# A leaky rectifier in place of a scaled copy in the decoding of float64 weights, and one VectorE instruction less

## The chip, the cores and the metric

The kernel runs on one core of one Trainium2 chip. The metric is the device time of one execution in microseconds (us), as the median of several runs. The engines are named as in the profile: PE is TensorE (PEld its weight loads), DVE is VectorE, ACT is ScalarE, POOL is GpSimd, SP is SyncE, which only issues transfers here.

## The reference

A windowed attention with a linear bias per head is followed by a feed-forward network with an approximate GELU. The weights of the network are float64; everything else is float32.

```python
# q, k, v: (8 batches, 8 heads, 576 positions, 64), float32
scores = scale * np.matmul(q, k.transpose(0, 1, 3, 2))
mask = (rel >= 0) & (rel < 128)              # rel = row - column
scores = np.where(mask, scores + bias[None], -1000000000.0)
attn = softmax(scores)                       # written out in the reference
out = np.matmul(attn, v)
x = out.transpose(0, 2, 1, 3).reshape(4608, 512)
h = x @ w_in                                 # (512, 2048), float64
g = h * (1.0 / (1.0 + np.exp(-1.702 * h)))
return g @ w_out                             # (2048, 512), float64
```

## The kernel before

**Feed-forward.** The 4608 rows of x are cut into 18 chunks of 256. The hidden width of 2048 is cut into 16 groups of 128. One step of a `Job` works on one chunk and one group: `up` multiplies x by a group of w_in into `h_ps` (line 553), ScalarE takes the tanh (line 558), VectorE makes g (line 559), ScalarE and GpSimd split g into a high and a low part, `gh` and `gl` (lines 562 and 563), and `down` multiplies these by a group of w_out into two accumulators `acc` (line 572). Each operand is held as a high part and the rest, so there are three products for one: 12 matmuls in `up`, 6 in `down`.

**Attention.** It runs as a pipeline of units; `tick` starts the next stage of several units. In the first two batches a unit is whole (`WholeUnit`): scores into `s_ps` and `sb_ps` (line 325), bias and row minimum on VectorE (line 352), exponentials on ScalarE (line 375), the sums' reciprocal `rec` on VectorE (lines 393 and 394), scaling of the probabilities `pb` by it on GpSimd and ScalarE (lines 403 and 400), transposes into `t_ps` (line 420), copies to `pw` (line 428), and the product with v into `x_ps` (line 477). `s_ps` has one buffer, so the next unit's scores wait until line 352 has read the last ones.

**Decoding.** The weights come in as float64, 32 tiles of 128x512 values: one of w_in and one of w_out for each of the 16 groups, in the order in which the groups are needed. `fetch` loads a tile through SP's queue (line 155). `decode` turns it into a float32 in `wc` and splits that into a high and a low part. A float64 is seen as two 32-bit words. The upper word, read as a float32, has the sign, the upper 8 bits of the 11-bit exponent, and then the other 3 bits of it and 20 of the fraction. ScalarE scales it by 2^-112 (line 211), which lowers the exponent field by 112; VectorE shifts the lower word right by 29 bits (line 212), shifts the scaled word left by 3 and joins the two (line 213): the exponent field then has the wanted value and the fraction 23 bits, but the sign has been shifted out. Line 214 takes the sign from the upper word and joins it. ScalarE rounds to the high part (line 217) and GpSimd subtracts for the low part (line 218). `wc` has three buffers, which it shares with another small tile.

**Order.** The program writes 24 steps in which the 32 tiles are decoded, at a pace that follows from when each group is needed, and mixes in the ticks of the attention. The order on each engine is then set by a scheduler that models each instruction's time. What is pinned keeps its written order: SP's loads, TensorE's idle matmuls at the start, and the first 8 decoded tiles. Each engine works through its queue in order, so an instruction that waits holds up all that stands behind it.

Of the kernel before, what the change touches and what calls it, by code (L numbers as in the profile page):

```python
# [8 lines left out]
F32 = mybir.dt.float32  # L9
# [4 lines left out]
AF = mybir.ActivationFunctionType  # L14
ALU = mybir.AluOpType
# [127 lines left out]
def tile_kernel(ctx: ExitStack, tc: tile.TileContext, q0, k0, v0, qT, kT, v, w_in, w_out, out):  # L143
    nc = tc.nc
# [58 lines left out]
    def decode(st, name, pin=lambda ins: ins):  # L203

        words = st.bitcast(I32).rearrange("p (m two) -> p m two", two=2)
        top, low = words[..., 1], words[..., 0]
        c = ffn.tile([P, 512], I32, name="wc", tag="o", bufs=3)

        pin(nc.scalar.activation(c.bitcast(F32), top.bitcast(F32), AF.Copy, scale=2.0 ** -112))
        pin(nc.vector.tensor_scalar(low, low, 29, None, ALU.logical_shift_right))  # L212
        pin(nc.vector.scalar_tensor_tensor(c, c, 3, low, ALU.logical_shift_left, ALU.bitwise_or))  # L213
        pin(nc.vector.scalar_tensor_tensor(c, top, -0x80000000, c, ALU.bitwise_and, ALU.bitwise_or))  # L214
        w = c.bitcast(F32)
        res = const.tile([P, 2, 512], F32R, name=name, tag=name)
        pin(nc.scalar.copy(res[:, 0], w))
        pin(nc.gpsimd.tensor_tensor(res[:, 1], w, res[:, 0].bitcast(F32), ALU.subtract))
        return res
# [425 lines left out]
    def decode_next():  # L645
        nonlocal halves
        g, ws = halves // 2, (w1, w2)[halves % 2]

        pin = [tc.keep_in_program_order] if halves < PINNED else []
        ws[g] = decode(ws[g], f"w{1 + halves % 2}_{g}", *pin)  # L650
        halves += 1
# [123 lines left out]
```

## Time and profile before

| | |
|---|---|
| time, median of 3 runs | 1074.23 us (1074.23 to 1074.42) |
| span of the profiled execution | 1072.5 us; the rest of its time, start and end outside the span, is not shown apart |
| mean granted clock of TensorE | 0.991 |
| PE busy | 1053.5 us, 98% of the span |
| DVE, ACT, POOL busy | 687.3, 595.2 and 610.8 us |
| line 214 | 32 instructions, 673 to 2394 ns, median 694, from 21.9 to 142 us |
| all of `decode` | 32 tiles, from 17.5 to 147 us |

Rows of busy time in a stretch read: start and end in us, length, then for each engine its busy time in us with the number of instructions, then the granted clock (1.00 is full speed), the share of the transfer engines that is busy, and GB/s. Rows in order of time read: start, length, engine, line, operation, output and inputs, and in brackets how long the engine was idle before it and what ended that. Rows by line give the shortest, median and longest duration in ns, and the first and the last start. Buffer numbers are left out of names there, so `rw` is any tile of raw weights.

### The profile page before, as it was taken

The page shows a single profiled execution, that of the slowest core. Times are in us where ns is not written, and L with a number is a line of the kernel's source. Part 1 is how long each engine was busy: PE and PEld are TensorE (multiplying, and loading weights), DVE is VectorE, ACT ScalarE, POOL GpSimd, SP SyncE. Part 2 cuts the span into 40 slices and gives each one's busy share as a digit, 9 for nine tenths or more (in the row PEclk, how much of TensorE's full clock was granted, in tenths as well). Part 3 has the DMA queues.
Part 4 walks back from the last instruction along what each step waited for, and adds up shares of the span by engine and source line. Part 5 has one row for each costly group of instructions (what it writes and reads, how often), then busy time and mean ns, then how long its engine had stood idle before and what let it go on. Part 6 is the DMA issues. An engine that isn't in the chain of part 4 may idle for free.

```text
span 1072.5 us, 21419 instructions
## 1 busy us (share of the span) xinstructions
PE 1053.5 (98%) x7041; PEld 931.5 (87%) x7041; DVE 687.3 (64%) x2149; ACT 595.2 (56%) x1811; POOL 610.8 (57%) x863
## 2 busy tenths in 40 slices
PE   9888999999999999999999999999999999999998
PEld 5656777899999999999999999999999999999987
DVE  6899843647896777654667668767877687413121
ACT  6869954546665565444555555655665556322222
POOL 3669954556675666554656557656666565323222
PEclk9889999999999999999999999999999999999999
DMA  8861112312223132202222213222222221000000
GB/s 309 305 231 54 44 30 75 83 38 77 75 80 85 51 86 75 62 16 67 58 76 54 70 53 90 75 60 71 82 65 85 57 77 28 20 2 20 1 21 20
DMA packets 88110, 78.45 MB, mean 73 GB/s; under 512 B 36800, under 2 KB 79296, under 8 KB 88000
## 3 DMA queue, kind: packets, MB, share of 16 engines
q1 hardware_dynamic: 82240, 67.14, 21.7%
q10 hardware_dynamic: 5760, 9.96, 2.5%
q8 instruction: 55, 0.90, 0.4%
q14 instruction: 55, 0.45, 0.1%
HBM read 67.63 MB, written 9.44 MB: 72 GB/s over the span
## 4 chain that ended last, share of the span: by engine, by line
PE 92%; DVE 4%; ACT 1%; DMA 1%; issue 0%; POOL 0%; SPq 0%; DVEq 0%; POOLq 0%; ACTq 0%
PE acc L572 37%; PE h_ps L553 37%; PE s_ps L335 5%; PE x_ps L500 5%; PE t_ps L443 4%; PE x_ps L477 1%; DVE wc L214 1%; DVE wc L213 1%; PE t_ps L420 1%; PE sb_ps L325 1%; DVE rw L212 1%; ACT pb L375 1%; PE s_ps L325 1%; DMA rw<-w_out 1%; DVE pb L352 0%; PE acc L189 0%
## 5 line engine op out<-in xcount | busy, mean ns | idle before, releaser
L563 POOL TENSOR_TENSOR gl<-g,gh 128x256 fp32r<-128x256 f32 x288 | 219.7, 763 | 284.1 <-ACT gh L562 220.0
L553 PE MATMUL h_ps<-xh,w 128*128 128x256 f32 x2304 | 370.2, 284 | 1.5 <-DVE g L559 1.0
L553 PEld LDWEIGHTS h_ps<-xh,w 128*128 128x128 f32 x2304 | 329.2, 189 | 33.2 <-DVE g L559 2.0
L572 PE MATMUL acc<-w,gh 128*128 128x512 f32 x1152 | 326.7, 401 | 0.5 <-ACT gh L562 0.5
L558 ACT ACTIVATE g<-h_ps 128x256 f32<-128x256 f32 x288 | 110.0, 382 | 237.5 <-PE h_ps L553 213.3
L559 DVE SCALAR_TENSOR_TENSOR g<-g,h_ps 128x256 f32<-128x256 f32 x288 | 119.4, 415 | 190.6 <-ACT g L558 189.3
L572 PEld LDWEIGHTS acc<-w,gh 128*128 128x128 f32 x1152 | 196.9, 189 | 28.2 <-ACT gh L562 1.1
L553 PE MATMUL h_ps<-xl,w 128*128 128x256 f32 x1152 | 196.1, 281 | 0.0
L562 ACT CAST gh<-g 128x256 fp32r<-128x256 f32 x288 | 116.5, 405 | 137.7 <-DVE g L559 127.0
L572 PE MATMUL acc<-w,gl 128*128 128x512 f32 x576 | 187.6, 401 | 0.1
L553 PEld LDWEIGHTS h_ps<-xl,w 128*128 128x128 f32 x1152 | 165.2, 189 | 6.7 <-issue 0.3
L313 POOL TENSOR_TENSOR K<-rk,K 128x384 fp32r<-128x384 f32 (+1 forms) x120 | 109.1, 909 | 75.0 <-ACT Q L293 14.3
L382 ACT ACTIVATE pb<-pb,mins 128x256 f32<-128x256 f32 (+2 forms) x216 | 105.0, 487 | 40.7 <-DVE mins L363 39.6
L572 PEld LDWEIGHTS acc<-w,gl 128*128 128x128 f32 x576 | 92.6, 189 | 10.5 <-issue 2.2
L407 DVE TENSOR_SCALAR pb<-pb,rec 128x256 f32<-128x256 f32 (+2 forms) x216 | 94.5, 473 | 3.3
L312 POOL TENSOR_TENSOR Q<-rq,Q 64x256 fp32r<-64x256 f32 (+1 forms) x120 | 82.8, 690 | 22.3 <-DVE g L559 3.3
L363 DVE CUSTOM_DVE_ANT_0 pb<-s_ps,bias 128x256 f32<-128x256 f32 (+3 forms) x240 | 85.7, 377 | 11.1 <-PE s_ps L335 9.8
L393 DVE TENSOR_SCALAR rec<-sums 128x2 f32<-128x2 f32 (+3 forms) x144 | 47.7, 331 | 57.6 <-ACT pb L382 52.9
L335 PE MATMUL s_ps<-K,Q 128*128 128x256 f32 (+1 forms) x432 | 80.2, 289 | 0.0
L311 DVE CAST K<-rk 128x384 fp32r<-128x384 f32 (+1 forms) x120 | 51.4, 428 | 44.6 <-PE s_ps L335 39.4
L462 DVE TENSOR_TENSOR pl<-t_ps,ph 128x512 fp32r<-128x512 f32 (+2 forms) x120 | 72.2, 604 | 8.3 <-ACT ph L456 4.5
L443 PE MATMUL t_ps<-ident,pb 128*128 128x128 f32 x408 | 73.9, 272 | 0.0
(69 smaller groups left out, 1354.9 us busy)
## 6 DMA issues: line engine op xcount, KB each, us to landing
rk<-kT SPq DMA_DIRECT2D x72, 192.0 KB, 2.5
rq<-qT SPq DMA_DIRECT2D x96, 128.0 KB, 2.4
out<-o ACTq DMA_DIRECT2D x36, 256.0 KB, 2.1
rw<-w_in SPq DMA_DIRECT2D x16, 512.0 KB, 6.2
rw<-w_out SPq DMA_DIRECT2D x16, 512.0 KB, 7.0
rk<-kT SPq DMA_DIRECT2D x48, 128.0 KB, 2.3
rv<-v SPq DMA_DIRECT2D x96, 64.0 KB, 2.0
rq<-q SPq DMA_DIRECT2D x16, 128.0 KB, 2.2
```

The costliest lines, as they stand in the source:

```text
L313: nc.gpsimd.tensor_tensor(K2, rk, K1.bitcast(F32), ALU.subtract)
L335: nc.tensor.matmul(u.s[:b.rows, e, b.first:b.end], u.Q[:, b.q0 - u.q0:b.q0 - u.q0 + b.rows], k[:, ko:ko + b.end - b.first], start=(z == 0) ...
L363: nc.vector.tensor_tensor_reduce(b.p[ra:rb, cs:b.end], u.s[ra:rb, e, cs:b.end], bias[head][ra:rb, cs:b.end], -SCALE, BIG, ALU.add, ALU.min ...
L382: nc.scalar.activation(live, live, AF.Exp, bias=u.mins[:b.rows, e:e + 1], scale=-1.0, accum_out=u.sums[:b.rows, e:e + 1],)
L407: nc.vector.tensor_scalar(live, live, u.rec[:rows, e:e + 1], None, ALU.mult)
L443: nc.tensor.transpose(u.t[:c.n, w:w + b.rows], b.p[:b.rows, col:col + c.n], ident[:b.rows, :b.rows])
L553: nc.tensor.matmul(h, w1[f][:, z, k * P:(k + 1) * P], x[:, k], start=(n == 0), stop=(n == len(ops) - 1))
L558: nc.scalar.activation(g, h, AF.Tanh, scale=0.851)
L559: nc.vector.scalar_tensor_tensor(g, g, 1.0, h, ALU.add, ALU.mult)
L562: nc.scalar.copy(gh, g)
L563: nc.gpsimd.tensor_tensor(gl, g, gh.bitcast(F32), ALU.subtract)
L572: nc.tensor.matmul(acc, g[:, t * P:(t + 1) * P], w2[f][:, z], start=(f == self.f0 and n == 0), stop=(f == self.f1 - 1 and n == 2))
```

## The change

ScalarE's first step uses a leaky rectifier instead of a copy: a positive word is scaled by 2^-112 as before, a negative one by 2^-112 times 2^32, so its exponent field is 32 higher. Shifted left by 3, this bit lands in the place of the sign. So the sign comes through the shift, and VectorE's third instruction is dropped.

```diff
-        pin(nc.scalar.activation(c.bitcast(F32), top.bitcast(F32), AF.Copy, scale=2.0 ** -112))
+        pin(nc.scalar.activation(c.bitcast(F32), top.bitcast(F32), AF.Prelu, scale=2.0 ** -112, alpha=2.0 ** 32))
         pin(nc.vector.tensor_scalar(low, low, 29, None, ALU.logical_shift_right))
         pin(nc.vector.scalar_tensor_tensor(c, c, 3, low, ALU.logical_shift_left, ALU.bitwise_or))
-        pin(nc.vector.scalar_tensor_tensor(c, top, -0x80000000, c, ALU.bitwise_and, ALU.bitwise_or))
         w = c.bitcast(F32)
```

Since the scheduler sets the order, other instructions move too. In the rows below an instruction is named by its line, operation, output and inputs; `rw_7_519` is a raw tile of group 7, and the last number only tells buffers apart (a group's tile of w_in has the lower one). After the change all lines behind 213 have a number lower by one: 352 is 351, 325 is 324, 553 is 552. A row of line 352 with the output `mins` alone reads out the row minimum.

VectorE before, around the wait for the weights of group 7 (43.5 us in the trace of before):

```order
L352 ISA pb,mins<-s_ps,bias_74 64x192
L352 ISA mins 64x1
L212 TENSOR_SCALAR rw_7_519<-rw_7_519 128x512
L213 SCALAR_TENSOR_TENSOR wc<-wc,rw_2_205 128x512
L393 TENSOR_SCALAR rec<-sums 128x4
L214 SCALAR_TENSOR_TENSOR wc<-rw_2_205,wc 128x512
L212 TENSOR_SCALAR rw_2_207<-rw_2_207 128x512
L394 RECIPROCAL rec<-rec 128x4
L212 TENSOR_SCALAR rw_7_521<-rw_7_521 128x512
L352 ISA pb,mins<-s_ps,bias_76 64x192
```

The same place after the change:

```order
L351 ISA pb,mins<-s_ps,bias_74 64x192
L351 ISA mins 64x1
L213 SCALAR_TENSOR_TENSOR wc<-wc,rw_2_205 128x512
L212 TENSOR_SCALAR rw_2_207<-rw_2_207 128x512
L212 TENSOR_SCALAR rw_7_517<-rw_7_517 128x512
L392 TENSOR_SCALAR rec<-sums 128x4
L393 RECIPROCAL rec<-rec 128x4
L212 TENSOR_SCALAR rw_7_519<-rw_7_519 128x512
L351 ISA pb,mins<-s_ps,bias_76 64x192
```

The steps on group 2 (line 213, and line 212 on its second tile) now stand ahead of line 212 on group 7, and line 214 is gone; behind that wait only the reciprocal and the second tile of group 7 are left ahead of the next reading of `s_ps`.

TensorE before, at the same time (from 43.2 us in the trace of before; `w_2_578` is the decoded first tile of group 2):

```order
L325 MATMUL s_ps<-rk,rq 64x192
L325 MATMUL sb_ps<-rk,rq 64x192
L477 MATMUL x_ps<-pw,VV 64x128 x2
L477 MATMUL x_ps<-pw,VV 64x256 x2
L477 MATMUL x_ps<-pw,VV 64x128 x2
L325 MATMUL s_ps<-rk,rq 64x192
L553 MATMUL h_ps<-xh,w_2_578 128x256 x4
L420 MATMUL t_ps<-ident,pb 128x128 x8
```

And after the change:

```order
L324 MATMUL s_ps<-rk,rq 64x192
L324 MATMUL sb_ps<-rk,rq 64x192
L476 MATMUL x_ps<-pw,VV 64x128
L324 MATMUL s_ps<-rk,rq 64x192
L552 MATMUL h_ps<-xh,w_2_573 128x256 x4
L419 MATMUL t_ps<-ident,pb 128x128 x2
L476 MATMUL x_ps<-pw,VV 64x128
L476 MATMUL x_ps<-pw,VV 64x256 x2
L476 MATMUL x_ps<-pw,VV 64x128 x2
L419 MATMUL t_ps<-ident,pb 128x128 x6
```

The third score product of this place has moved ahead of nearly all of the `x_ps` products, and the first products with the weights of group 2 with it.

VectorE before, from 59.3 us in the trace of before, behind a reciprocal that GpSimd waits for:

```order
L394 RECIPROCAL rec<-rec 64x2
L213 SCALAR_TENSOR_TENSOR wc<-wc,rw_3_260 128x512
L213 SCALAR_TENSOR_TENSOR wc<-wc,rw_4_318 128x512
L214 SCALAR_TENSOR_TENSOR wc<-rw_3_260,wc 128x512
L393 TENSOR_SCALAR rec<-sums 64x2
L212 TENSOR_SCALAR rw_11_739<-rw_11_739 128x512
L214 SCALAR_TENSOR_TENSOR wc<-rw_4_318,wc 128x512
L394 RECIPROCAL rec<-rec 64x2
L213 SCALAR_TENSOR_TENSOR wc<-wc,rw_4_320 128x512
L352 ISA pb,mins<-s_ps,bias_80 64x192
L352 ISA mins 64x1
L212 TENSOR_SCALAR rw_11_741<-rw_11_741 128x512
```

After the change, from the reciprocal of the same unit:

```order
L393 RECIPROCAL rec<-rec 64x2
L213 SCALAR_TENSOR_TENSOR wc<-wc,rw_4_320 128x512
L212 TENSOR_SCALAR rw_11_729<-rw_11_729 128x512
L351 ISA pb,mins<-s_ps,bias_80 64x192
L351 ISA mins 64x1
L392 TENSOR_SCALAR rec<-sums 64x2
L558 SCALAR_TENSOR_TENSOR g<-g,h_ps 128x256
L393 RECIPROCAL rec<-rec 64x2
L212 TENSOR_SCALAR rw_11_731<-rw_11_731 128x512
L213 SCALAR_TENSOR_TENSOR wc<-wc,rw_5_379 128x512
```

The two tiles of group 4 and the second of group 3 were decoded behind this reciprocal; now only one of line 213 and one of line 212 stand between it and the next unit's reading of `s_ps`.

## The prediction

> **What bounds the kernel now.** I read the busy shares first, then busy time by stretch, then the waits of TensorE, and last the instructions in order of time where it waits. All times are of one profiled execution with a span of 1072.5 us; the runs' median is 1074.23, so 1.7 us lie around the span and I take them as unchanged. The first fence is the page's first part, the second busy time in three stretches (start and end, length, then the busy time of each engine, the clock and the DMA share).
>
> ```profile
> PE 1053.5 (98%) x7041; PEld 931.5 (87%) x7041; DVE 687.3 (64%) x2149; ACT 595.2 (56%) x1811; POOL 610.8 (57%) x863
> ```
> ```profile
> 0.00:43.50 43.50, 39.17 (x261) 25.54 (x261) 32.37 (x123) 33.60 (x105) 20.54 (x30) 1.00 0.84 285
> 43.50:106.00 62.50, 53.71 (x310) 38.01 (x306) 57.68 (x130) 48.04 (x147) 49.80 (x37) 0.86 0.54 186
> 106.00:1072.50 966.50, 960.60 (x6474) 867.93 (x6474) 597.28 (x1898) 513.61 (x1561) 540.47 (x796) 1.00 0.20 56
> ```
> Over the span TensorE is the bound, but not in the middle row: there it stands idle for 62.50 - 53.71 = 8.8 us, while VectorE is busy for 57.68 of 62.50, and the clock is 0.86. That is where the weights are decoded beside the first attention and feed-forward steps. After 106 us TensorE is busy for 960.60 of 966.50, so what is won before 106 stays won. The same stretch cut into thirds, and below it the busy time of line 214's instructions alone (second number, with their count):
>
> ```profile
> 43.50:55.00 11.50, 8.99 (x47) 6.69 (x43) 7.68 (x24) 6.95 (x19) 8.94 (x6) 0.70 1.01 390
> 55.00:75.00 20.00, 16.21 (x88) 11.21 (x88) 19.87 (x36) 13.02 (x42) 14.40 (x10) 0.74 0.74 254
> 75.00:106.00 31.00, 28.51 (x178) 20.11 (x178) 30.13 (x72) 28.06 (x87) 26.46 (x21) 1.00 0.23 67
> ```
> ```profile
> 43.50:55.00 11.50, 1.37 (x2) 0.70 1.01 390
> 55.00:75.00 20.00, 7.29 (x6) 0.74 0.74 254
> 75.00:106.00 31.00, 9.07 (x9) 1.00 0.23 67
> ```
> The instruction that goes holds VectorE for 1.37 + 7.29 + 9.07 = 17.73 us there, in 17 of its 32 executions. In the last two thirds VectorE is never free (19.87 of 20, 30.13 of 31); in the first it is free for a third, and the DMA share of 1.01 says that weights are still arriving.
>
> The clock falls in whole blocks. Cut at 3.41 us, the rows are (TensorE's busy time is the second number, the clock the third from the right):
>
> ```profile
> 43.84:47.25 3.41, 1.84 (x17) 1.18 (x16) 3.41 (x14) 1.89 (x5) 1.35 (x2) 1.00 1.02 407
> 47.25:50.66 3.41, 2.46 (x12) 2.06 (x11) 3.26 (x10) 2.50 (x11) 3.41 (x2) 0.50 1.02 414
> 50.66:54.07 3.41, 3.41 (x13) 2.98 (x13) 0.70 (x1) 2.03 (x5) 3.41 (x4) 0.50 1.06 379
> ...
> 60.89:64.30 3.41, 1.53 (x17) 1.17 (x17) 3.41 (x9) 1.90 (x7) 3.41 (x2) 1.00 1.03 378
> 64.30:67.71 3.41, 3.40 (x14) 2.06 (x14) 3.41 (x3) 2.01 (x8) 3.36 (x4) 0.50 0.13 37
> 67.71:71.12 3.41, 2.16 (x6) 1.73 (x7) 3.41 (x7) 2.06 (x8) 1.62 (x1) 0.50 0.73 203
> 71.12:74.53 3.41, 3.41 (x21) 2.70 (x19) 3.34 (x5) 2.02 (x5) 2.37 (x2) 0.50 1.03 377
> ```
> Twice a block in which TensorE works for about half (1.84, 1.53 of 3.41) is followed by blocks at half clock: two the first time, three the second. Work at half clock takes twice as long, so the loss is half of the busy time there: (2.46 + 3.41) / 2 = 2.9 us and (3.40 + 2.16 + 3.41) / 2 = 4.5 us. With the idle time the most that can be won is, by thirds: 2.5 + 2.9 = 5.4, 3.8 + 4.5 = 8.3, and 2.5; in all 16.2 us. The waits of TensorE from 43 to 110 us (total, times, longest):
>
> ```profile
> PE t_ps L420 <- POOL pb L403: 3.9, 5, 1.9
> PE s_ps L325 <- DVE mins L352: 2.0, 2, 1.6
> PE t_ps L420 <- ACT w L217: 1.3, 1, 1.3
> ```
> None names line 214. It acts through what stands behind it on VectorE, and through GpSimd.
>
> **The step on ScalarE.** Line 211 stays one instruction on 128x512 elements; only its function changes. By line over the whole run (shortest, median, longest in ns), then three groups on ScalarE (busy, mean ns):
>
> ```profile
> L211 ACT ACTIVATE wc<-rw x32: 646/672/700, 19.2 to 137.6; 128x512 f32<-128x512 f32 x32
> L213 DVE SCALAR_TENSOR_TENSOR wc<-wc,rw x32: 661/691/1775, 19.9 to 139.2; 128x512 int32<-128x512 int32 x32
> L214 DVE SCALAR_TENSOR_TENSOR wc<-rw,wc x32: 673/694/2394, 21.9 to 141.3; 128x512 int32<-128x512 int32 x32
> L217 ACT CAST w<-wc x32: 602/621/672, 23.3 to 142.3; 128x512 fp32r<-128x512 f32 x32
> ```
> ```profile
> L382 ACT ACTIVATE pb<-pb,mins 128x256 f32<-128x256 f32 x168 | 84.7, 505 | 34.5 <-DVE mins L363 33.7
> L400 ACT ACTIVATE pb<-pb,rec 128x256 f32<-128x256 f32 x24 | 11.3, 506 | 2.8 <-DVE rec L394 2.8
> L375 ACT ACT_TABLE_LOAD x1 | 1.3, 1283 | 2.6 <-issue 2.6
> ```
> An exponential (line 382) takes 505 ns and a scaled copy (line 400) 506 ns on the same shape, so I expect the rectifier at the copy's 672 ns: cost nothing. Bounds: the plain cast of that shape, 621 (17 x 0.05 = 0.9 us won), and two exponentials of half the width, 1010 (17 x 0.34 = 5.8 us more on ScalarE in the stretch, where it has 62.5 - 48.0 = 14.5 free, though only 2.9 of them after 75 us). It needs no wait that the copy did not have, and no DMA moves: SP's queue is the same row by row, and no GpSimd transfer exists here.
>
> **The step on VectorE.** Removed are 32 instructions. Where nothing is in the way, one moves the next start by 0.61 us; where something is, it takes up to 2.39. The next fence shows both, VectorE and GpSimd in order of time (start, length).
>
> ```profile
> 59.33 1.26 DVE L213 SCALAR_TENSOR_TENSOR wc<-wc,rw 128x512 int32<-128x512 int32 x2
> 60.52 0.67 DVE L214 SCALAR_TENSOR_TENSOR wc<-rw,wc 128x512 int32<-128x512 int32 x1
> 61.13 0.15 DVE L393 TENSOR_SCALAR rec<-sums 64x2 f32<-64x2 f32 x1
> ...
> 63.07 2.70 DVE L212 TENSOR_SCALAR rw<-rw 128x512 int32<-128x512 int32 x1
> ...
> 66.01 2.19 DVE L214 SCALAR_TENSOR_TENSOR wc<-rw,wc 128x512 int32<-128x512 int32 x1
> ```
> ```profile
> 59.51 4.00 POOL L403 TENSOR_SCALAR pb<-pb,rec 64x192 f32<-64x192 f32 x1 [0.45 <-DVE rec L394]
> 63.48 1.26 POOL L218 TENSOR_TENSOR w<-wc,w 128x512 fp32r<-128x512 f32 x1
> 64.72 0.76 POOL L403 TENSOR_SCALAR pb<-pb,rec 64x192 f32<-64x192 f32 x1
> 65.45 1.52 POOL L218 TENSOR_TENSOR w<-wc,w 128x512 fp32r<-128x512 f32 x1
> ```
> The scaling of line 403 takes 0.76 us at 64.72 and 4.00 at 59.51, beside VectorE's unbroken row of decoding; it ends when that row does, and TensorE's 1.9 us wait in the list hangs on it. The other way round, line 212 at 63.07 stands 2.70 us until GpSimd's two instructions are over, and line 214 at 66.01 ends as GpSimd's next ends. So the two engines shut each other out, and of line 214's 17.73 us only 17 x 0.61 = 10.4 is its own work: by thirds 1.2, 3.7 and 5.5. The rest, 7.3 us, is GpSimd's time, which another decoding instruction will meet. I take 0.61 each, and keep 17.73 for the lower end.
>
> The Trainium skill (SBUF — State Buffer, "Who interferes with whom") says that a VectorE instruction with two SBUF inputs and a GpSimd instruction that reads SBUF exclude each other for the whole instruction, whichever starts first. By it line 214 gives back 10.4 us, by the plain busy time 17.73. The trace agrees with the page as far as the 4.00 against 0.76 us go.
>
> What this is worth, third by third:
> - 0 to 43.5 us: nothing. Four executions go, but VectorE ends this stretch in a 1.63 us wait for weights:
>
> ```profile
> 43.52 0.43 DVE L212 TENSOR_SCALAR rw<-rw 128x512 int32<-128x512 int32 x1 [1.63 <-DMA rw<-w_in]
> ...
> 44.58 0.69 DVE L214 SCALAR_TENSOR_TENSOR wc<-rw,wc 128x512 int32<-128x512 int32 x1
> ...
> 45.92 0.34 DVE L352 CUSTOM_DVE_ANT_0 pb<-s_ps,bias 64x192 f32<-64x192 f32 x1
> ```
> - 43.5 to 55: behind that wait TensorE's score product stands until line 352 at 45.92 has read the scores. In the new order two decoding steps come ahead of the wait and line 214 is gone, so line 352 is due about 0.61 + 0.34 + 0.61 = 1.5 us sooner (a line 213 and a line 212 moved ahead, line 214 gone), unless the second half of the weights holds it. But TensorE's new order asks for that product before most of the x_ps products, so the gap moves forward rather than vanishing. The reciprocal that lets GpSimd start line 403 also comes 1.5 us sooner; that should fill the block from 47.25, so that the clock returns one block earlier (3.41 / 2 = 1.7 us). I take 2.0; bounds 0 and 5.4.
> - 55 to 75: VectorE's queue is the bound. Its 6 executions give 3.7 us, and the starved scaling at 59.51 starts among fewer instructions, which shortens the gap that brought the second half-clock stretch (4.5 us); I count a fifth of that, 0.8. Sum 4.5; bounds 3.7 less what ScalarE may take (2 us), and 8.3.
> - 75 to 106: 9 executions, 5.5 us, but TensorE has only 2.5 us to win and ScalarE is busy for 28.06 of 31. I take 1.5; bounds 0 and 2.5.
> - After 106: TensorE is full. The 11 executions up to 145 lie beside it and cost or give nothing; if the new order opened a gap it would show here (plus or minus 1).
>
> Sum: 0 + 2.0 + 4.5 + 1.5 + 0 = 8.0 us. Span 1064.5, median 1066.2.
>
> **Rivals.**
> - All of it: both half-clock stretches and the gaps go. For it: two gaps of 1.6 and 1.9 us bring all of the 7.4 us of clock. Against: the DMA wait at 43.5 stays. 1074.2 - 16.2 = 1058; from 1062 down I count this case.
> - The wait is passed on: lines 212 and 213 meet GpSimd where line 214 did, and after 75 us ScalarE (28.06 of 31) and GpSimd (26.46) are nearly full. Then the clock stays as it is, and only some 0.5 of the 5.5 us after 75 and half of the 3.7 before arrive: 2.4 us, 1071.8.
> - Slower: VectorE's queue now runs ahead of the loads. Line 212 of weight groups 7 to 11 stands ahead of the score step, and between 43.5 and 55 the DMA share is 1.01, so it comes no earlier; TensorE meets each such wait sooner, in a gap of over 1.5 us per block. Two more blocks at half clock than now cost 2 x 1.7 = 3.4 us, with nothing gained elsewhere: 1077.6. It decides once VectorE waits in line 212 for over 1.5 us at three places instead of one.
> - The change does not do what it says: the rectifier is not in the loaded function table. With two loads for each of 32 steps at 1.283 us this is 82 us: 1156. Against it, the changed program has one load in ScalarE's order, ahead of the first exponential, as before. The Trainium skill (ScalarE: Activation LUTs, "What ACT_TABLE_LOAD costs") puts a switch at about 2.66 us with its drain, which would make 170; no run here shows a second load.
>
> **How the numbers follow.** Forecast 0.60 (gain 4 to 12), all of it 0.14, passed on 0.16, slower 0.08, no table 0.02. A measurement of this kernel tells about 0.2% from no change, 2.15 us, so 1072.1 is the edge: of the passed-on case about two thirds lies below it, 0.11; faster 0.85, same 0.06 (the rest of it and a little of the slower case), slower 0.09. The range from 1058.5 to 1072 leaves out about 0.15 above and 0.04 below; the forecast's own is 1062 to 1070.
>
> **What would show it.** Right: no group for the third instruction, VectorE's total down by 20 to 31 us; line 211 at 650 to 700 ns; line 403's longest well under 4.00; TensorE's idle time from 43.5 to 100 us down from 8.8 to about 5; fewer blocks at 0.50 than five; TensorE full after about 98. Wrong: line 211 above 800 ns; five or more half-clock blocks; VectorE's DMA waits above 4 us between 43 and 56 us; new gaps of TensorE after 110.

## The result, and the profile after

The changed kernel took 1067.87 us (median of 4 runs, 1064.2 to 1068.36) against 1074.23: a ratio of 0.9922, 95% interval 0.9896 to 0.9948. In a second set of runs it took 1064.58 (1064.23 to 1065.22), ratio 0.9895, interval 0.9872 to 0.9917. One disturbed run (1694.32 us, of the old order without the third instruction, below) is left out of all ratios. In later sets the kernel before itself spread from 1072.4 to 1082.1, so ratios below are each to the kernel before in the same set.

The profiled execution after took 1068.36 us, the slowest of the four, with a span of 1066.3. Line numbers behind 213 are lower by one. First the page's busy shares, then the busy time in the three stretches and in the three thirds of the middle one, columns as before.

```profile
PE 1052.9 (99%) x7041; PEld 929.1 (87%) x7041; DVE 660.5 (62%) x2117; ACT 597.2 (56%) x1811; POOL 603.5 (57%) x863
```
```profile
0.00:43.50 43.50, 38.76 (x232) 24.61 (x234) 29.89 (x117) 31.85 (x99) 20.07 (x30) 0.94 0.80 272
43.50:106.00 62.50, 58.77 (x372) 41.95 (x369) 51.24 (x130) 54.63 (x169) 48.95 (x43) 0.96 0.59 204
106.00:1066.30 960.30, 955.41 (x6442) 862.57 (x6440) 579.36 (x1872) 510.70 (x1544) 534.46 (x791) 1.00 0.20 56
```
```profile
43.50:55.00 11.50, 10.71 (x71) 7.49 (x68) 8.49 (x24) 8.86 (x24) 6.75 (x6) 0.93 1.03 393
55.00:75.00 20.00, 18.12 (x114) 12.68 (x112) 18.04 (x40) 15.19 (x48) 15.01 (x13) 0.91 0.75 252
75.00:106.00 31.00, 29.94 (x190) 21.79 (x191) 24.71 (x68) 30.57 (x98) 27.18 (x26) 1.00 0.33 103
```
VectorE's total is 26.8 us lower. In the middle stretch TensorE is busy for 58.77 us instead of 53.71, at a clock of 0.96 instead of 0.86, and VectorE is no longer full: what is full after 75 us is ScalarE, 30.57 of 31. But the first stretch got worse: TensorE's busy time fell from 39.17 to 38.76 and the clock from 1.00 to 0.94. The next fence has the main ones of TensorE's waits from 43 to 110 us (total, times, longest). Then come ScalarE's first step and the scaling on GpSimd (shortest, median, longest in ns), and VectorE's two decoding steps (busy time, mean in ns, idle time before them).

```profile
PE t_ps L419 <- DVE mins L351: 1.9, 2, 1.1
PE h_ps L552 <- POOL w L217: 0.6, 1, 0.6
...
PE t_ps L419 <- POOL pb L402: 0.4, 1, 0.4
```
```profile
L211 ACT ACTIVATE wc<-rw x32: 654/682/722, 19.3 to 125.8; 128x512 f32<-128x512 f32 x32
```
```profile
L402 POOL TENSOR_SCALAR pb<-pb,rec x40: 597/924/1471, 8.6 to 198.8; 128x256 f32<-128x256 f32 x20, 128x128 f32<-128x128 f32 x12, 64x192 f32<-64x192 f32 x8
```
```profile
L213 DVE SCALAR_TENSOR_TENSOR wc<-wc,rw 128x512 int32<-128x512 int32 x32 | 32.4, 1017 | 9.5 <-ACT wc L211 9.4
L212 DVE TENSOR_SCALAR rw<-rw 128x512 int32<-128x512 int32 x32 | 18.0, 570 | 4.2 <-DMA rw<-w_in 3.8 <-DMA rw<-w_out 0.4
```
The scaling that took 4.00 us is gone (longest 1.47), and of the 3.9 us in which the transposes waited for GpSimd 0.4 are left. The rectifier has a median of 682 ns against the copy's 672. VectorE now waits 9.4 us for ScalarE ahead of line 213, and 4.2 us for weights in line 212 (3.1 before).

The loss in the first stretch is one place. VectorE and TensorE of the changed kernel in order of time:

```profile
32.79 0.94 DVE L212 TENSOR_SCALAR rw<-rw 128x512 int32<-128x512 int32 x1 [2.30 <-DMA rw<-w_in]
...
34.08 0.43 DVE L212 TENSOR_SCALAR rw<-rw 128x512 int32<-128x512 int32 x1 [0.35 <-DMA rw<-w_out]
34.43 0.42 DVE L351 CUSTOM_DVE_ANT_0 pb<-s_ps,bias 128x256 f32<-128x256 f32 x1
...
35.25 0.70 PE L324 MATMUL s_ps<-rk,rq 64*128 64x256 f32 x2 [1.50 <-DVE mins L351]
...
37.75 0.48 PE L324 MATMUL sb_ps<-rk,rq 64*128 64x256 f32 x1 [1.09 <-ACT pw L427]
```
Line 212 on the weights of group 5 stands ahead of line 351 in VectorE's queue and waits 2.30 and 0.35 us for its transfer; the scores wait behind it, and TensorE stands idle for 1.50 us. The new order is not the reason: in the kernel before, the same two executions of line 212 stand ahead of the same score step, but the first of them found its weights there and the second waited 0.84 us. The second gap of TensorE, 1.09 us, is not new either; it was 1.24 us before, at full clock:

```profile
30.63 0.42 DVE L212 TENSOR_SCALAR rw<-rw 128x512 int32<-128x512 int32 x1
...
31.98 0.57 DVE L212 TENSOR_SCALAR rw<-rw 128x512 int32<-128x512 int32 x1 [0.84 <-DMA rw<-w_out]
32.46 0.40 DVE L352 CUSTOM_DVE_ANT_0 pb<-s_ps,bias 128x256 f32<-128x256 f32 x1
...
36.05 0.48 PE L325 MATMUL sb_ps<-rk,rq 64*128 64x256 f32 x1 [1.24 <-ACT pw L428]
```
In the changed kernel the clock is at half from 38.3 us on:

```profile
38.60:42.01 3.41, 3.41 (x11) 2.23 (x11) 3.36 (x9) 3.41 (x10) 3.41 (x3) 0.50 0.38 76
42.01:43.50 1.49, 1.49 (x7) 0.86 (x8) 1.49 (x3) 1.41 (x5) 1.28 (x2) 0.50 0.85 300
...
58.90:62.30 3.40, 3.40 (x20) 2.77 (x20) 3.16 (x9) 3.06 (x8) 1.91 (x2) 0.52 1.01 360
```
Half clock lasts until about 45.2 and comes once more from 58.8 to 62.2: 10.2 us of it in all, three blocks, where before there were 17.1 us, five blocks.

### The profile page after: what moved, and what is told of

Its sections match the earlier page's. It is cut to its first block, busy times and chain, and to the rows that moved or that the text cites. A ratio compares the mean times of both kernels' runs of the same rounds, so it can differ in the third digit from the quotient of the medians.

```text
span 1066.3 us, 21362 instructions
## 1 busy us (share of the span) xinstructions
PE 1052.9 (99%) x7041; PEld 929.1 (87%) x7041; DVE 660.5 (62%) x2117; ACT 597.2 (56%) x1811; POOL 603.5 (57%) x863
## 4 chain that ended last, share of the span: by engine, by line
PE 94%; DVE 3%; ACT 1%; DMA 1%; issue 1%; POOL 0%; SPq 0%; DVEq 0%; POOLq 0%; ACTq 0%
PE h_ps L552 38%; PE acc L571 37%; PE s_ps L334 5%; PE x_ps L499 5%; PE t_ps L442 4%; PE x_ps L476 2%; PE t_ps L419 1%; PE sb_ps L324 1%; PE s_ps L324 1%; DVE wc L213 1%; DMA rw<-w_out 1%; ACT pb L374 1%; DVE rec L392 0%; PE acc L189 0%; DVE rw L212 0%
## 5 line engine op out<-in xcount | busy, mean ns | idle before, releaser
L406 DVE TENSOR_SCALAR pb<-pb,rec 128x256 f32<-128x256 f32 (+2 forms) x216 | 91.8, 461 | 3.2
```

The costliest lines, as they stand in the source:

```text
L406: nc.vector.tensor_scalar(live, live, u.rec[:rows, e:e + 1], None, ALU.mult)
```

## The experiments

Two ways of making kernels are used. In one the scheduler sets the order as usual; in the other the order of TensorE, VectorE, ScalarE and GpSimd is written out, so that only the wanted difference is left:

```diff
+        for engine, packed in ORDER.items():
+            ...
+            for a, b in zip(order, order[1:]):
+                tc.add_manual_dep(
+                    mine[b], mine[a].name,
+                    mybir.DependencyInfo(mybir.DependencyClass.NoSync, mybir.DependencyReason.DATA),
+                    reason="set_order")
```
Such kernels have higher line numbers: the rectifier or copy is line 219, the shift 220, the join 221, and a third instruction 222.

**Does writing the order out cost anything?** The kernel before, with its own order written out.

> The kernel before, with each engine's order written out as in the other kernels with a fixed order, and nothing else changed. If fixing the order costs nothing by itself: 1.000 of before, within 0.002. If it costs, the kernels with a fixed order are to be read against this one: 1.002 would be all that the new order with the third instruction showed above before.

Measured: 1076.18 us (1073.05 to 1081.01), ratio 1.0004, 0.9986 to 1.0022. It costs nothing that shows.

**The rectifier alone.** The third instruction stays; the order on every engine is that of the kernel before.

```diff
-        ... AF.Copy, scale=2.0 ** -112))
+        ... AF.Prelu, scale=2.0 ** -112, alpha=2.0 ** 32))
```


> The kernel before with the rectifier in place of the copy; the third instruction stays and joins a sign that is already there, and the order is that of before. If the rectifier costs what the copy costs: 1074.2 within 1.0. If its 10 ns more (682 against 672 in the traces) are on the path: up to 0.3 more. If it helps in itself: under 1072.

Measured: 1075.79 us, ratio 1.0001, 0.998 to 1.0023. ScalarE's line and the middle stretch:

```profile
L211 ACT ACTIVATE wc<-rw x32: 655/674/705, 19.2 to 138.4; 128x512 f32<-128x512 f32 x32
```
```profile
43.50:106.00 62.50, 52.79 (x309) 37.36 (x309) 58.37 (x128) 47.53 (x147) 48.56 (x37) 0.86 0.54 187
```
The rectifier takes 674 ns, and the stretch looks as before (52.79 busy, clock 0.86). The function costs nothing and gains nothing beyond the interval, some 0.2% either way.

**The third instruction left out, with the copy.** The order is that of the changed kernel; the signs of the weights are lost.

```diff
-        pin(nc.vector.scalar_tensor_tensor(c, top, -0x80000000, c, ALU.bitwise_and, ALU.bitwise_or))
```


> The changed kernel with the copy instead of the rectifier: the signs of the weights are lost, the work and the order are those of the changed kernel. 1064 to 1068.5 us, as the changed kernel itself, by both theories; it is a second sample of its spread of 4 us, and if its profile shows the weights of group 5 landing before 33 us, the early wait of the changed kernel is chance of the transfers and not its order.

Measured: 1064.53 us (1063.16 to 1067.23), ratio 0.9888, 0.9859 to 0.9917. So the whole change of time comes with leaving out the third instruction, the new order included. In this run the first stretch had no loss, in the same order as the changed kernel:

```profile
25.00:43.50 18.50, 17.34 (x116) 11.72 (x114) 14.47 (x48) 17.98 (x53) 10.96 (x11) 1.00 0.81 272
```
The changed kernel's first profile has 15.82 busy at 0.86 there. That loss is therefore not fixed by the order; it comes and goes from one execution to the next. So does the landing of the transfers: the weights of group 5, waited for until 32.79 us there, were in place at 30.06 here. Later this run, too, has three blocks at half clock, 10.2 us.

**Order or instruction?** The scheduler moved much else when the third instruction went. Two kernels part the two: before's order without the third instruction (with the rectifier), and the changed kernel's order with copy and third instruction, put right behind each line 221.

> The changed program, with every engine's queue forced into the order that the kernel before has, the dropped instruction taken out of it. Theory A, the gain is VectorE's shorter queue: it is there in this order too, and the early loss (VectorE standing 2.3 us for the weights of group 5 ahead of a score step) is not, so 1062 to 1068 us. Theory B, the gain is the scheduler's new order: 1072 to 1074.5.

> The kernel before (copy and third instruction), with every queue forced into the order of the changed kernel, the third instruction put right behind its line 213. Theory A: the work is back, so no gain, 1074 to 1079 us (with the early loss of the new order). Theory B: the order is what gains, 1066 to 1070.

Measured: the first has a ratio of 0.9895 (0.9861 to 0.9928), the second 1078.46 us, 1.0022 (1.0000 to 1.0043). The first kernel's early and middle stretch, the middle stretch of the second, then the third instruction and GpSimd's scaling in the second:

```profile
25.00:43.50 18.50, 16.28 (x91) 10.62 (x91) 13.42 (x45) 15.39 (x45) 11.41 (x12) 0.83 0.77 257
43.50:106.00 62.50, 59.12 (x371) 42.05 (x370) 50.26 (x129) 54.66 (x173) 48.82 (x44) 0.97 0.57 196
```
```profile
43.50:106.00 62.50, 52.72 (x304) 37.33 (x302) 59.86 (x127) 47.01 (x148) 44.18 (x38) 0.86 0.54 188
```
```profile
L222 DVE SCALAR_TENSOR_TENSOR wc<-rw,wc x32: 691/1101/3649, 20.7 to 140.6; 128x512 int32<-128x512 int32 x32
L411 POOL TENSOR_SCALAR pb<-pb,rec x40: 594/922/1648, 8.6 to 207.7; 128x256 f32<-128x256 f32 x20, 128x128 f32<-128x128 f32 x12, 64x192 f32<-64x192 f32 x8
```
The whole gain comes in the old order, and none in the new order with the instruction. The order is not the source. Two more things can be read here. The early loss, which I expected not to come in the old order, is there as well (16.28 busy, clock 0.83), though TensorE's longest gap there, 1.26 us, is that of the kernel before (1.24), which kept its full clock. And the second kernel has no scaling over 1.65 us, yet gains nothing: to be rid of the scaling of 4.00 us alone does not gain the time.

**Is it linear?** Before's order, rectifier, third instruction twice.

```diff
+        pin(nc.vector.scalar_tensor_tensor(c, top, -0x80000000, c, ALU.bitwise_and, ALU.bitwise_or))
```


> The rectifier, and the third instruction twice in a row (both join a sign that is there), all queues in the order of the kernel before. Theory A, VectorE's queue from 43 to 106 us is the bound, and each third instruction costs its 0.61 us there: the step from one to two costs as much as the step from none to one saved (11 us), 1083 to 1090 us. Rival, the first one only filled waits that are there anyway: under 1079.

Measured: 1088.03 us, ratio 1.0104, 1.0083 to 1.0125. From none to one is 1.05% (1 - 0.9895), from one to two 1.04%: some 11 us each, more than the 8 that I worked out.

**Its length, or its kind?** In the old order the third instruction is replaced by one with a single input: a maximum over each row, written to the row's first element, which it overwrites. So the first of 512 values is lost, and ScalarE's cast still waits for it.

```diff
-        pin(nc.vector.scalar_tensor_tensor(c, top, -0x80000000, c, ALU.bitwise_and, ALU.bitwise_or))
+        pin(nc.vector.tensor_reduce(c.bitcast(F32)[:, 0:1], c.bitcast(F32), mybir.AxisListType.X, ALU.max))
```


> The rectifier, and in place of the third instruction one that keeps VectorE about as long but reads only one input from on-chip memory: a maximum over the 512 values of the tile, written over its first value (so one of 512 values in each row of the weights is wrong). Order of the kernel before. If the length of VectorE's queue is all: 1074 to 1077 us, as before. If the gain comes from GpSimd being no longer shut out by an instruction with two inputs: 1064 to 1067, as without it. If both count: between, 1068 to 1073.

Measured: 1068.43 us (1067.03 to 1070.24), ratio 0.9921, 0.9898 to 0.9944. Its durations, the page's shares, the middle stretch, GpSimd's scaling, and TensorE's wait for it in the middle stretch:

```profile
L222 DVE TENSOR_REDUCE wc<-wc x32: 662/680/687, 21.9 to 136.2; 128x1 f32<-128x512 f32 x32
```
```profile
PE 1049.5 (98%) x7041; PEld 929.0 (87%) x7041; DVE 680.0 (64%) x2149; ACT 593.6 (56%) x1811; POOL 603.5 (57%) x863
```
```profile
43.50:106.00 62.50, 55.22 (x345) 39.47 (x343) 59.87 (x142) 51.92 (x162) 50.59 (x43) 0.95 0.57 196
```
```profile
L411 POOL TENSOR_SCALAR pb<-pb,rec x40: 593/921/3237, 8.6 to 176.6; 128x256 f32<-128x256 f32 x20, 128x128 f32<-128x128 f32 x12, 64x192 f32<-64x192 f32 x8
```
```profile
PE t_ps L428 <- POOL pb L411: 2.3, 2, 1.9
```
One such instruction takes 680 ns against 694 for line 214 by the medians, VectorE has as many of them, and it is as full in the middle stretch (59.87 of 62.50). The totals differ more, 21.7 against 30.8 us, since some executions of line 214 are stretched, up to 2394 ns. Yet 0.79% of the time, 8.5 us, is regained. Against no third instruction at all (0.9895) it costs 0.26% by the medians, 3 us, and by the two intervals nothing to some 7 us, where the one with two inputs costs 1.05%, 11 us. So by the medians the length of VectorE's queue by itself is about a quarter of the price; by the intervals it can be anything from none to two thirds. The rest hangs on something else in which the two instructions differ. TensorE's idle time in the middle stretch hardly fell (8.8 to 7.3 us), and its longest wait for GpSimd is still 1.9 us; what fell is the time at half clock, from 17.1 us to 6.8. That goes beyond one profile: five kernels with the two-input instruction (before, its order written out, the rectifier alone, the new order, twice) had 17.1, 27.3, 17.1, 17.1 and 34.1 us at half clock up to 110 us, the kernels without it 10.2 at most; only the kernel before with shifts in turn, below, falls out of this with 6.8. Against the kernel before VectorE's and GpSimd's totals are each 7.3 us lower (687.3 to 680.0 and 610.8 to 603.5) at the same number of instructions. The Trainium skill (SBUF — State Buffer, "Who interferes with whom") has an instruction with at most one SBUF input, outside the two-port modes, not contend with GpSimd. The trace agrees: 662 to 687 ns, never longer, against line 214's 673 to 2394. All this fits the two engines shutting each other out, but doesn't prove it as the cause of the 8.5 us: a scaling still stretches to 3.24 us here, and this instruction also leaves the raw tile alone, which so comes free sooner, and writes one column only. The three weren't told apart.

**Line 212 ahead of the loads.** The early loss of the changed kernel led to line 212 being held behind line 213 of the tile before, in the changed kernel and in the kernel before; the scheduler orders the rest.

```diff
+    joined = []
...
-        pin(nc.vector.tensor_scalar(low, low, 29, None, ALU.logical_shift_right))
-        pin(nc.vector.scalar_tensor_tensor(c, c, 3, low, ALU.logical_shift_left, ALU.bitwise_or))
+        shift = pin(nc.vector.tensor_scalar(low, low, 29, None, ALU.logical_shift_right))
+        in_turn(joined[-1:] + [shift])
+        joined.append(pin(nc.vector.scalar_tensor_tensor(c, c, 3, low, ALU.logical_shift_left, ALU.bitwise_or)))
```


> The changed kernel, with line 212 of each tile held behind line 213 of the tile ahead of it, so that VectorE no longer stands in line 212 for late weights with a score step behind it. If those waits (3.8 + 0.4 us in the changed kernel's trace, 4.8 in the one with the copy) and the half-clock stretch behind the first are a loss of the order: 1059 to 1064 us. Rival, line 212 ahead of its turn fills time that VectorE has free and the decoding now comes later: 1066 to 1071.

> The kernel before with the same rule for line 212. If the waits for weights are a loss of their own: 1070 to 1074 us, 2 to 4 less than before. Rival, VectorE's queue is so full that it gains nothing by it: 1075 to 1079.

Measured: the changed kernel with shifts in turn 1065.88 us, ratio 0.9896 (0.9875 to 0.9918); the kernel before with them 1074.65 us, 0.9984 (0.9968 to 0.9999). Both lie between what the two theories asked for. In the first, the early loss is gone:

```profile
25.00:43.50 18.50, 18.07 (x120) 12.10 (x120) 12.48 (x48) 18.44 (x54) 12.29 (x12) 1.00 0.90 299
```
But 10.2 us at half clock come later, as much as in the changed kernel's first profile, and much else in its order differs, since the scheduler was free. In the second only two blocks are at half clock, but TensorE idles later instead, 8.1 of 31 us:

```profile
75.00:106.00 31.00, 22.90 (x148) 17.51 (x148) 28.59 (x63) 26.22 (x80) 24.29 (x22) 0.98 0.15 42
```
**Steady cost or chance?** No edit: the changed kernel and the one with shifts in turn again, side by side.

> The changed kernel a second time, beside the kernel with the shifts in turn. If its early waits in line 212 are a steady cost, it lies some 2.5 us above the kernel with shifts in turn again, at 0.992 of before. If they are chance of the transfers, its runs spread over some 4 us and the two kernels' intervals overlap.

> The changed kernel with line 212 held behind the line 213 of the tile before, a second time. Steady-cost theory: 0.989 to 0.990 of before, runs within 2.5 us of each other, and below each median of the changed kernel. Chance theory: no difference to the changed kernel beyond the interval.

Measured: 1064.58 us (ratio 0.9895, 0.9872 to 0.9917) and 1065.76 us (0.9904, 0.9882 to 0.9927). The two don't differ beyond their intervals, so the early waits are no steady cost, and holding the shifts back in the scheduler's order gains nothing that shows. The spread of some 4 us that the chance of the transfers should bring is not seen within this set (1064.23 to 1065.22), only between the two sets. The changed kernel's profile in this set, its longest waits in line 212, two gaps of TensorE and the stretches:

```profile
27.73 0.43 DVE L212 TENSOR_SCALAR rw<-rw 128x512 int32<-128x512 int32 x1 [2.65 <-DMA rw<-w_in]
...
37.90 0.46 DVE L212 TENSOR_SCALAR rw<-rw 128x512 int32<-128x512 int32 x1 [1.84 <-DMA rw<-w_in]
...
45.46 0.54 PE L324 MATMUL s_ps<-rk,rq 64*64 64x192 f32 x2 [1.08 <-DVE mins L351]
...
53.72 0.30 PE L419 MATMUL t_ps<-ident,pb 64*128 64x64 f32 x2 [1.86 <-DVE mins L351]
```
```profile
25.00:43.50 18.50, 16.72 (x111) 11.36 (x110) 12.97 (x46) 16.49 (x50) 10.32 (x10) 1.00 0.76 248
43.50:106.00 62.50, 57.71 (x372) 42.07 (x372) 51.06 (x127) 56.49 (x176) 51.10 (x46) 0.97 0.57 197
```
Line 212 waits as much or more (2.65 and 1.84 us), but the clock stays at 1.00 up to 55 us; only one block, from 55.8 to 59.2, is at half, behind the gap of 1.86. With 3.4 us at half clock in place of 10.2 the span is 1062.6 in place of 1066.3. The kernel with the copy had a span of 1062.6 as well, in the same order and with 10.2 us at half clock, so these blocks alone don't set the span.

**The old order, in turn.** No third instruction, every engine in the order of before, but on VectorE each line 212 (220 here) that stood ahead of the join of the tile before is moved right behind it, 25 tiles in all. No diff is shown: only VectorE's written order differs.

> Rectifier, no third instruction, every engine in the order of the kernel before except that on VectorE each line 212 that stood ahead of line 213 of the tile before is moved right behind it (25 tiles). If running ahead of the loads costs in that order too, it is at or below the old order without the third instruction: 0.987 to 0.9895 of before. If the shifts done early were a reserve that shortened the chain from a load to its weights later, TensorE idles in 75 to 106 us instead, and it lies 2 us or more above: 0.9915 or more.

Measured: 1060.86 us (1060.70 to 1062.08), ratio 0.9864, 0.9839 to 0.9888. The slowest of its runs is faster than the fastest of the changed kernel (1064.20), so this version beats both. Against the old order without this move (0.9895, in another set) the intervals overlap, though its slowest run lies below that kernel's fastest (1063.61). The three stretches, and VectorE's shift:

```profile
0.00:43.50 43.50, 39.90 (x269) 26.14 (x271) 29.77 (x120) 34.09 (x107) 20.72 (x32) 1.00 0.87 298
43.50:106.00 62.50, 58.95 (x383) 41.96 (x380) 52.20 (x130) 56.95 (x180) 53.38 (x47) 1.00 0.55 187
106.00:1058.60 952.60, 948.20 (x6396) 858.60 (x6394) 583.30 (x1869) 501.34 (x1527) 526.88 (x786) 1.00 0.20 56
```
```profile
L220 DVE TENSOR_SCALAR rw<-rw 128x512 int32<-128x512 int32 x32 | 23.6, 738 | 0.0
```
The clock is 1.00 throughout, and line 220 waits for no transfer. TensorE's idle time in the middle (3.55 us) is that of the changed kernel (3.73): what it wins is the clock, and the first stretch. That comes near the case called "all of it" in the prediction (1058): both half-clock stretches are gone, though not all of the gaps. It did not come with the change alone.

## Why the prediction was right

The time fell where it was forecast. Counted are, as in the prediction, the idle time of TensorE and half of its busy time at half clock (in the first profile of after (3.41 + 1.49) / 2 up to 43.5, 1.7 / 2 from there to 45.2, and 3.40 / 2 at 58.9; in the second 3.41 / 2), in us:

| stretch | before | after, first profile | gain | after, second profile | gain | predicted |
|---|---|---|---|---|---|---|
| 0 to 43.5 | 4.33 | 4.74 + 2.45 | -2.9 | 4.38 | -0.1 | 0 |
| 43.5 to 55 | 2.51 + 2.94 | 0.79 + 0.85 | 3.8 | 2.97 | 2.5 | 2.0 |
| 55 to 75 | 3.79 + 4.49 | 1.88 + 1.70 | 4.7 | 1.21 + 1.71 | 5.4 | 4.5 |
| 75 to 106 | 2.49 | 1.06 | 1.4 | 0.60 | 1.9 | 1.5 |
| after 106 | 5.90 | 4.89 | 1.0 | 4.84 | 1.1 | 0 |

The rows of the second profile, of the changed kernel in the second set of runs:

```profile
0.00:43.50 43.50, 39.12 (x259) 25.27 (x259) 29.99 (x122) 33.18 (x104) 20.31 (x30) 1.00 0.83 282
43.50:55.00 11.50, 8.53 (x57) 5.80 (x56) 11.01 (x27) 9.69 (x29) 7.65 (x7) 1.00 1.02 396
55.00:75.00 20.00, 18.79 (x126) 13.56 (x124) 18.02 (x39) 15.96 (x52) 15.00 (x14) 0.91 0.85 291
75.00:106.00 31.00, 30.40 (x191) 22.70 (x192) 22.03 (x63) 30.85 (x99) 28.45 (x27) 1.00 0.22 63
106.00:1062.60 956.60, 951.76 (x6415) 859.23 (x6413) 579.11 (x1870) 506.73 (x1535) 529.72 (x788) 1.00 0.20 56
```
The first profile sums to 8.0, while the spans differ by 6.2. The other 1.8 us stay unexplained: the ends of matmuls are modelled, and halving busy time is coarse. So in that execution the sum came out near partly by luck, because misses cancel: the early stretch on the one side, the next third and the 1.0 at the end on the other. In the second no stretch is more than 1.1 us from its forecast, and the sum is 10.8; the spans differ by 9.9. The forecast of 8.0 lies between the two executions.

- **ScalarE's step, nothing.** Shown: 682 ns in the changed kernel, 674 with the third instruction kept, and a ratio of 1.0001 for the function alone. The rival of a table that has to be loaded is out.
- **0.61 us each, and the rest passed on.** This is the step that failed. VectorE's total fell by 26.8 us, where 32 x 0.61 would be 19.5, and all of line 214's time 30.8: so some 4 us were passed on, not 11.3. Line 213 took 3.2 us more (29.2 to 32.4). The price of the instruction is 11 us in the old order, none to one as one to two, and by the medians with the single-input instruction most of it is not queue length. I had the mutual shutting out in view and used it only to take something off the gain, where the traces point to it, without proving it, as the larger part.
- **0 to 43.5, nothing.** Wrong in the first profile, by 2.9 us. I looked only at the wait that ends the stretch, at 43.5, and not at line 212 on group 5, which stands ahead of a score step in both orders. It is the rival "slower" in small, VectorE's queue ahead of the loads with a gap of 1.50 us and two blocks at half clock, but it is of that execution and not of the new order: the second profile and the kernel with the copy, in the same order, don't have the loss, and the old order without the third instruction has it. Its point of decision, three waits of over 1.5 us, was not what counts: the second set had waits of 2.65 and 1.84 us at full clock before 43.5. What a wait costs depends on the gap that it leaves on TensorE, by what stands behind it.
- **43.5 to 55.** The gain is 3.8 in the first profile and 2.5 in the second, not 2.0. In neither does a half-clock stretch begin here; I had allowed for one block less, not for none. That is no steady gain: the kernel with the copy, in the same order, has a gap of 2.00 us at 45.2 and a block at half clock behind it.
- **55 to 75 and 75 to 106.** As forecast, 4.7 and 1.4 (5.4 and 1.9 in the second profile). The scaling of 4.00 us is gone, but the 0.8 us that I counted for it has no support: the new order with the instruction lost that scaling too and gained nothing, and the single-input instruction kept one of 3.24 us and regained 8.5. After 75 us ScalarE is full (30.57 of 31) and VectorE is not (24.71), as the 2.9 us left free on ScalarE had said. The 5.5 us of line 214 there could not arrive, and did not.
- **After 106, nothing.** 1.0 and 1.1 us came, at the edge of the 1 us that I allowed.

Both medians, 1067.87 and 1064.58, lie in the forecast's own range. Of the signs named, line 211 (682), the idle time in the middle (8.8 to 3.7), the total of VectorE (26.8) and three blocks instead of five came as written.

## What to carry to other kernels

When an instruction goes from a full engine, its worth need not be its own duration: ask which engine it may shut out, and try a single-input instruction of the same length in its place. Where an engine waits in order, look at every wait for a transfer in the new order and at what stands behind it, not only at the longest one of the old trace. And once the freed engine is no longer the bound, work done ahead of need can cost: in the old order, moving the shifts behind the joins took the ratio from 0.9895 to 0.9864 (1060.86 us); in the order that the scheduler made, holding them back gained nothing that shows. And take more than one profile of a kernel before a loss is put down to its order.

## What was not expected of the hardware

The length of a gap on TensorE alone doesn't decide over the clock. In the changed kernel the gaps of 1.50 and 1.09 us brought two blocks at half clock in the first profile, and in the second 1.86 us brought one and 1.08 us none. Nor does TensorE's share of work in the block ahead, which was about half in the prediction's two cases. Cut at the edges of the blocks, the first row here (kernel before) was not followed by half clock, and the second (the kernel with the copy) was, though TensorE did more in it:

```profile
33.59:37.00 3.41, 2.17 (x14) 1.32 (x13) 3.38 (x10) 3.41 (x12) 1.10 (x2) 1.00 0.99 325
```
```profile
62.86:66.27 3.41, 2.43 (x18) 1.43 (x18) 3.41 (x3) 2.24 (x7) 2.81 (x3) 1.00 0.60 154
```
The Trainium skill (TensorE: Matmul & The Clock Gate, "What's actually happening") has a window of 4096 cycles, 3413 ns, that runs on freely, so that it varies from run to run where in it a gap falls. The stretches at half clock of 3.4, 6.8 and 10.2 us agree. By the same section the clock falls after at least one idle window, about 3.4 us. Here it fell with gaps of 1.50 and 1.86 us, and the measurement decides. What makes it fall stays open. The half-clock blocks are part of why one kernel spreads over 4 us: with three blocks at half clock the span was 1066.3, with one 1062.6. It is not all of it, since the kernel with the copy had three blocks and 1062.6. And two instructions with medians of 694 and 680 ns, with two inputs and with one, differ by 8.5 us at the end, which their medians do not tell; their totals, 30.8 and 21.7 us, differ by 9.1.
